# P written sorted by partition quarters, conversions by bit operations, a new order of stages, and eleven pairs transposed by VectorE

## The chip, the cores and the metric

The kernel runs on one core of a Trainium2 chip: TensorE (PE in the profile), VectorE (DVE), the scalar engine (ACT), GpSimd (POOL) and SyncE (SP), which issues all DMAs here. The metric is the device time of one execution in microseconds, lower is better. Before the change it was 659.45 us, the median of three runs (658.87 to 664.38).

## The reference

Three blocks stand in a row, all in float32, with B = 4, H = 12, S = 448, head width 64 and model width 768.

```python
# 1: causal attention, 48 heads
scores = (q @ k.T) / sqrt(64)                    # 448 x 448, -1e9 above the diagonal
x = softmax(scores) @ v                          # heads joined to (B, S, 768)
# 2: mixing
theta = x @ w_theta
y = w_tok_r @ (x * cos(theta)) + w_tok_i @ (x * sin(theta))
u = x + y;  x = u + relu(u @ w_ch)
# 3: four attention experts of width 64, two chosen per token by logits = x @ w_gate
out = sum over the two chosen e of  w_e * (softmax(scale * (x @ wq[e]) @ (x @ wk[e]).T) @ (x @ wv[e]) @ wo[e])
```

## The kernel before

Work is held with features on the partitions and the 448 tokens along the free dimension. Products that need float32 accuracy are made from a high and a low float32r part of each operand, three matmuls for one (`mm3`).

There are four stages for each batch b. `a` (`attn1`, line 753) is the attention of block 1, six pairs of heads. `m` (`mixing`, 794) is theta, sine and cosine, and the token matmuls of block 2. `p` (`project`, 857) is the product with w_ch and everything of block 3 that comes ahead of its scores: q, k, v and the gates. `c` (`attn2`, 962) is the attention of block 3, two pairs of experts, and the output product.

The attention of a pair is in `pair` (633). TensorE forms the scores in five PSUM banks of the tag tp. For each of seven pieces VectorE adds the mask and takes the row extreme (`softmax`, 646), ACT takes the exponential and its sum, and GpSimd or ACT scales with the reciprocal (`norm`, 673). The result is P, a tile `pa` of 128 x 2048, which is 16 blocks of 128 x 128. P must be transposed for the product with v. There are two ways. In the first TensorE transposes 16 blocks (`tp<-ident,pa`) and ACT or VectorE copies them out of PSUM to the tile `ph`. In the second (`by_dve`, for the pairs in the table `BYDVE`, nine before) VectorE transposes blocks of 32 x 32 in place, and 16 DMAs `ph<-pa` of 64 KB each move the blocks to their places, in runs of 32 elements, 128 bytes. The product P times V is `tp<-ph,vt` or `tp<-ph,v`.

The weights w_theta and w_ch and the token matrices arrive as float64. `widen` (570) makes a high and a low float32r half from the two 32-bit words of each number, for 24 halves of 384 columns (tile `c`) and 7 of 448 (tile `zt`). A converted half is kept in DRAM (`scr<-unit`) and loaded again for later batches (`unit<-scr`).

The order of the work is not written out. `Plan` records every operation; `Plan.issue` (322) then goes through time with assumed costs and issues on each engine the ready operation with the earliest due time. Due times come from the table `K`, the turn of each tile tag comes from `ORDER`, and where an operation has several engines to choose from (`either`, 283) the planner chooses. The instructions are emitted by one line, 498, so the profile is read by tile names. All engines go through their instructions in order.

Of the kernel before, what the change touches and what calls it, by code (L numbers as in the profile page):

```python
# [30 lines left out]
REBIAS = 2.0 ** -112  # L31
LOWBIT = 2.0 ** -52
NVG = E * D + E


class View:
# [16 lines left out]
    def rearrange(self, pattern, **sizes):  # L53
        left, right = (self._axes(side) for side in pattern.split("->"))
        known = dict(sizes)
        for group, n in zip(left, self.idx.shape):
            free = [a for a in group if a not in known]
            for a in free[:1]:
                known[a] = n // math.prod(known[x] for x in group if x != a)
        shape = [math.prod(known[a] for a in group) for group in right]  # L60
        return self._then(lambda ap: ap.rearrange(pattern, **sizes), self.idx.reshape(shape))

# [55 lines left out]
COLD = 7000.0  # L118
ISSUE = 380.0
SWITCH = 200.0  # L120
# [9 lines left out]
class Plan:  # L130
# [16 lines left out]
    def cost(self, engine, name, out, ins, kw):  # L147
# [14 lines left out]
        if engine == "vector":  # L162
            if name == "tensor_tensor_reduce":
                n = ins[0].width
            if name == "tensor_reduce":
                n = ins[0].width
            fast = name in ("tensor_scalar", "tensor_copy", "memset") and not psum and n >= 64
            return 68.0 + n * (0.521 if fast else 1.042)
# [130 lines left out]

    def scale(self, out, p, by):  # L300
        kw = {"scalar1": by, "scalar2": 1.0, "op0": OP.mult, "op1": OP.mult}
        self.either(("gpsimd", "tensor_scalar", (out, p), kw), ("scalar", "activation", (out, p, AF.Copy), {"scale": by}))

# [18 lines left out]
    def issue(self):  # L322
# [58 lines left out]
        count = 0  # L381
        port = dma_free = 0.0
        table = None
        mode = 0
        while count < len(self.steps):
# [13 lines left out]
            for e in order:  # L399
# [61 lines left out]
                if e == "sync":  # L461
                    dma_free = max(dma_free, end) + s.lag - 2200.0
                    done = dma_free + 2200.0
                s.at = (now, end)
                for u in s.heirs:
# [35 lines left out]
class Engine:  # L501
# [9 lines left out]
K = {"path": 2.0679528, "hop": -288.0949, "slack": 44.7258729, "war": 328.8541, "ahold": 262497.9943,  # L511
# [9 lines left out]


@with_exitstack
def dense_sparse_attention_kernel(ctx: ExitStack, tc: tile.TileContext, qk, v, w64, w32, wo, wvg, wtok, out):
# [9 lines left out]
    BUFS = {"unit": 6, "hl": 12, "zt": 6, "zn": 3, "xt": 2 * NK, "c1": 4, "raw": 3, "vt": 2,  # L534
            "qp": 3, "v2": 4, "pa": 2, "ph": 2, "cmb": 2, "st": 9, "gt": 2, "sm": 2}
    PBUFS = {"tp": 6, "mm": 2}
# [33 lines left out]
    def widen(raw, n, hi, lo, by=1.0):  # L570


        e_ = raw[:, :n, 1]
# [12 lines left out]
        plan.copy(hi, p_, "sgv")  # L586
        plan.combine(lo, p_, hi.f32(), OP.subtract, "gv")

# [44 lines left out]
    def pair(raw, vts, gate, dest, due, gap, by_dve):  # L633
# [9 lines left out]
        p_ = sbt([2048], F32, "pa")  # L643
        pc = p_[:, 768:1280]

        def softmax(sc_, p, n, m, col):
            dve.tensor_tensor_reduce(out=p, in0=sc_, in1=m, scale=-0.125, scalar=3.0e38,
                                     op0=OP.add, op1=OP.min, accum_out=bias[:, col:col + 1])
            act.activation(p, p, AF.Exp, bias=bias[:, col:col + 1], scale=-1.0, accum_out=sums[:, col:col + 1])

        def part(j, c):
            at = UNIT[c] * P + 128 * (c + 1) * j
            return p_[:, at:at + 128 * (c + 1)]

# [26 lines left out]
        got = scores()  # L681
        pool.memset(pc[:, S:], 0.0)
        soft(got, 2)
# [4 lines left out]
        plan.claim(p_)  # L688
        softmax(sc_[:, :S], pc[:, :S], S, mask3, 6)
        soft(got, 1)  # L690
        soft(got, 0)
        norm(2, 7, [(pc[:, :S], 6)] + [(part(j, c), 2 * (2 - c) + j) for c in (1, 0) for j in range(2)])
        plan.due = due + K["f2"] * gap

        pt = sbt([2048], F32, "ph")
        if by_dve:
            for at, n in ((0, 768), (768, 1280)):
                dve.transpose(p_[:, at:at + n], p_[:, at:at + n])
            plan.due = due + K["f4"] * gap
            for a in range(4):  # L700
                plan.group()
                for b_ in range(4):
                    block = p_.rearrange("p (u b k) -> p u b k", b=4, k=32)[32 * a:32 * a + 32, :, b_]
                    sp.dma_start(pt[32 * b_:32 * b_ + 32, 512 * a:512 * a + 512].rearrange("p (u q) -> p u q", q=32), block)
                plan.end_group()
# [6 lines left out]
        else:  # L712
# [3 lines left out]
            for i in range(4):  # L716
                tp = pst("tp")
                for n in range(4 * i, 4 * i + 4):
                    pe.transpose(tp[:, P * (n - 4 * i):P * (n - 4 * i + 1)], p_[:, P * n:P * n + P], ident)
                    if n == 0:  # L720
                        plan.claim(pt)
# [7 lines left out]

        plan.due = due + K["f3"] * gap  # L730
        o_ = pst("tp")
        hl = [sbt([S], F32R, "hl") for _ in range(2)] if dest is None else []
        plan.group()
# [305 lines left out]
```

## Time and profile before

| | |
|---|---|
| Median of three runs | 659.45 us (658.87 to 664.38) |
| Profiled execution | 663.81 us, span 662.0 us |
| TensorE / VectorE / ACT / GpSimd busy | 94% / 66% / 52% / 21% of the span |
| Granted TensorE clock, mean | 0.992 |
| DMA | 112.66 MB in 122,221 packets, 80,816 of them under 512 B |

Busy times are shares of the span, and the engines run beside each other, so they do not add up. The times of "idle before" count only the idle time of that engine just ahead of an instruction, and the name behind the arrow is what ended it. "SPq" is SyncE's issue of a DMA.

### The profile page before, as it was taken

The numbers are of one execution on the slowest core, as the hardware profiler recorded it, in microseconds if no ns is written. First come the engines' busy times: TensorE is split into PE (matmuls) and PEld (weight loads), VectorE is DVE, ScalarE is ACT, GpSimd is POOL, SyncE is SP. The second block draws the span as 40 slices with busy tenths as digits, with TensorE's granted clock in tenths as the row PEclk, the third lists the DMA queues.
The fourth block names the chain that finished last, engine by engine and source line by source line (L and its number), as shares of the span: only waits on it lengthen the run. The fifth ranks groups of instructions, "written<-read, shape, count | busy, mean of one in ns | idle before, by whom it ended". The sixth has DMA issues, their size and how long they took to land.

```text
span 662.0 us, 12525 instructions
## 1 busy us (share of the span) xinstructions
PE 621.5 (94%) x4352; PEld 535.4 (81%) x4352; DVE 435.4 (66%) x1319; ACT 345.6 (52%) x906; POOL 138.8 (21%) x252
## 2 busy tenths in 40 slices
PE   7989898999989999998889999989989999999987
PEld 5668577798879789887779889868879789999876
DVE  5989999943997986767442886656820768424260
ACT  5999898933362345756542552575721463101362
POOL 3465365401230011333120110113200120100010
PEclk9999999999999999998999999999999999999989
DMA  8667746204333787778778861267785873056325
GB/s 333 219 191 228 253 140 223 79 0 118 138 97 97 252 277 244 215 168 266 157 159 282 284 135 72 59 122 175 191 231 148 271 140 116 31 166 204 90 62 173
DMA packets 122221, 112.66 MB, mean 170 GB/s; under 512 B 80816, under 2 KB 92592, under 8 KB 122160
## 3 DMA queue, kind: packets, MB, share of 16 engines
q1 hardware_dynamic: 122160, 111.88, 57.4%
q8 instruction: 34, 0.56, 0.4%
q14 instruction: 27, 0.22, 0.1%
HBM read 81.15 MB, written 21.26 MB: 155 GB/s over the span
## 4 chain that ended last, share of the span: by engine, by line
PE 58%; DVE 15%; ACT 9%; SPq 7%; DMA 7%; issue 4%; POOL 0%; DVEq 0%; ACTq 0%; POOLq 0%
PE mm L498 42%; PE tp L498 17%; SPq L498 7%; ACT pa L498 6%; DVE zt L498 3%; DVE pa L498 3%; DVE cmb L498 3%; DMA unit<-scr 3%; DMA c<-scr 2%; DVE c L498 1%; DMA ph<-pa 1%; DMA out<-cmb 1%; DVE st L498 1%; DVE unit L498 1%; ACT ph L498 1%
## 5 line engine op out<-in xcount | busy, mean ns | idle before, releaser
L498 ACT ACTIVATE pa<-pa,st 128x128 f32<-128x128 f32 (+3 forms) x329 | 161.8, 516 | 56.4 <-DVE st L498 49.9
L498 PE MATMUL mm<-zt,unit 128*128 128x448 f32 x720 | 159.5, 374 | 1.9 <-DVE xt L498 1.9
L498 PEld LDWEIGHTS mm<-zt,unit 128*128 128x128 f32 x720 | 133.6, 188 | 18.2 <-issue 4.0
L498 PE MATMUL mm<-wt,zn 128*128 128x448 f32 x504 | 113.2, 373 | 2.4 <-ACT wt L498 1.2
L498 DVE CUSTOM_DVE_ANT_0 pa<-tp,mask 128x384 f32<-128x384 f32 (+3 forms) x224 | 87.9, 445 | 25.3 <-PE tp L498 25.2
L498 PEld LDWEIGHTS mm<-wt,zn 128*128 128x128 f32 x504 | 91.8, 188 | 12.2 <-DVE zn L498 1.6
L498 POOL TENSOR_SCALAR pa<-pa,st 128x384 f32<-128x384 f32 (+3 forms) x119 | 64.1, 554 | 170.2 <-DVE st L498 135.5
L498 PE MATMUL mm<-hl,unit 128*128 128x448 f32 x432 | 94.1, 373 | 2.8 <-DMA unit<-scr 1.1
L498 PEld LDWEIGHTS mm<-hl,unit 128*128 128x128 f32 x432 | 80.0, 188 | 13.8 <-ACT hl L498 1.5
L498 PE MATMUL tp<-raw 64*128 64x384 f32 (+3 forms) x336 | 63.6, 427 | 2.6 <-DVE st L498 1.1
L498 PE MATMUL tp<-ph,vt 128*64 128x128 f32 (+1 forms) x960 | 49.4, 264 | 12.9 <-issue 7.5
L498 PEld LDWEIGHTS tp<-ph,vt 128*64 128x64 f32 x960 | 45.8, 145 | 16.9 <-issue 8.7
L498 PE MATMUL tp<-ident,pa 128*128 128x128 f32 x368 | 50.9, 282 | 6.6 <-POOL pa L498 3.2
L498 PEld LDWEIGHTS tp<-ident,pa 128*128 128x128 f32 x368 | 43.0, 144 | 16.3 <-POOL pa L498 6.7
L498 PEld LDWEIGHTS tp<-raw 64*128 64x128 f32 (+1 forms) x336 | 34.9, 189 | 20.5 <-issue 4.3
L498 ACT ACTIVATE zn<-tp 128x512 fp32r<-128x512 f32 (+1 forms) x38 | 20.4, 546 | 52.5 <-PE tp L498 52.4
L498 ACT ACTIVATION_READ_ACCUMULATOR pa<-pa,st 128x1 f32 x224 | 42.3, 189 | 0.0
L498 DVE TENSOR_TENSOR zn<-tp,zn 128x512 fp32r<-128x512 f32 (+1 forms) x48 | 28.9, 620 | 16.9 <-ACT zn L498 16.6
L498 ACT ACTIVATE ph<-tp 128x512 f32<-128x512 f32 x62 | 33.2, 593 | 6.8 <-PE tp L498 6.6
L498 PE MATMUL mm<-unit,zt 128*128 128x260 f32 (+1 forms) x264 | 34.8, 286 | 0.5 <-DMA unit<-scr 0.3
L498 PEld LDWEIGHTS mm<-unit,zt 128*128 128x128 f32 (+1 forms) x264 | 33.1, 183 | 2.3 <-issue 1.0
L498 PE MATMUL tp<-hl,c 128*128 128x448 f32 x144 | 32.9, 372 | 1.3 <-DMA c<-scr 1.3
(115 smaller groups left out, 737.8 us busy)
## 6 DMA issues: line engine op xcount, KB each, us to landing
unit<-scr SPq DMA_DIRECT2D x96, 384.0 KB, 4.2
scr<-unit SPq DMA_DIRECT2D x32, 384.0 KB, 3.7
raw<-qk SPq DMA_DIRECT2D x24, 480.0 KB, 4.3
c<-w SPq DMA_DIRECT2D x24, 384.0 KB, 3.6
ph<-pa SPq DMA_DIRECT2D x144, 64.0 KB, 2.3
vt<-v SPq DMA_DIRECT2D x24, 256.0 KB, 3.6
unit<-scr SPq DMA_DIRECT2D x18, 260.0 KB, 3.2
c<-scr SPq DMA_DIRECT2D x18, 256.0 KB, 4.5
```

Source lines behind the costliest of these rows:

```text
L498: getattr(getattr(self.nc, engine), name)(*args, **kw)
```

## The change

It has five parts.

1. In a by_dve pair P is written sorted by partition quarters: the columns of the 16 blocks are laid out by their quarter of 32 first and by block second. VectorE then transposes two halves of 1024 columns (before 768 and 1280), and each of the 16 moves takes 512 contiguous elements of 32 partitions, runs of 2 KB. In such a pair the mask pass writes back into PSUM and the exponential reads from there; the 64 unused columns of the last block are filled in PSUM by VectorE, where GpSimd filled them in SBUF.
2. `widen` joins the bits of the two words by shift and or, where it made the mantissa with a multiply-add in PSUM and a multiply.
3. `ORDER` goes batch by batch (m1 behind c0, and so on), and `K` is new.
4. `BYDVE` has two more pairs, 3 and 5 of batch 1, eleven in all.
5. The planner's model: an issue costs 400 ns, at most 8 DMAs are on their way, a cost for transposes on VectorE. Pools: qp 3 to 2 buffers, v2 4 to 2, and a separate tag hc (4) for the output of block 3's attention.

```diff
-BYDVE = {"a0": (), "a1": (), "a2": (0, 2, 4), "a3": (0, 2, 4), "c0": (0,), "c1": (0,), "c2": (0,), "c3": ()}
-ORDER = ["a0", "m0", "a1", "m1", "p0", "c0", "a2", "p1", "m2", "c1", "a3", "p2", "m3", "c2", "p3", "c3"]
+BYDVE = {"a0": (), "a1": (3, 5), "a2": (0, 2, 4), "a3": (0, 2, 4), "c0": (0,), "c1": (0,), "c2": (0,), "c3": ()}
+ORDER = ["a0", "m0", "a1", "p0", "c0", "m1", "a2", "p1", "c1", "m2", "a3", "p2", "c2", "m3", "p3", "c3"]
...
-        dve.tensor_scalar(p_.bitcast(U32), e_, 3, 0x7F800000, op0=OP.logical_shift_left, op1=OP.bitwise_and)
+        u_ = p_.bitcast(U32)
+        dve.tensor_scalar(u_, e_, 3, 0x7FFFFFFF, op0=OP.logical_shift_left, op1=OP.bitwise_and)
         plan.claim(hi)
-        dve.scalar_tensor_tensor(p_.bitcast(U32), e_, 0x80000000, p_.bitcast(U32), op0=OP.bitwise_and, op1=OP.bitwise_or)
-        dve.tensor_scalar(e_, e_, 0xFFFFF, None, op0=OP.bitwise_and)
-        x_ = pst("tp")[:, :n]
-        act.activation(x_, e_, AF.Copy, scale=by * 2.0 ** -20, bias=by)
-        y_ = e_.bitcast(F32)
-        dve.scalar_tensor_tensor(y_, raw[:, :n, 0].bitcast(U32), by * LOWBIT, x_, op0=OP.mult, op1=OP.add)
-        plan.combine(p_, y_, p_, OP.mult, "vg")
-        plan.copy(hi, p_, "sgv")
-        plan.combine(lo, p_, hi.f32(), OP.subtract, "gv")
+        dve.scalar_tensor_tensor(u_, r_, 29, u_, op0=OP.logical_shift_right, op1=OP.bitwise_or)
+        dve.scalar_tensor_tensor(u_, e_, 0x80000000, u_, op0=OP.bitwise_and, op1=OP.bitwise_or)
+        if by == 1.0:
+            plan.copy(hi, p_, "sgv")
+            plan.combine(lo, p_, hi.f32(), OP.subtract, "gv")
+        else:
+            plan.scale(hi, p_, by, "sgv")
+            dve.scalar_tensor_tensor(lo, p_, by, hi.f32(), op0=OP.mult, op1=OP.subtract)
...
+        by_key = p_.rearrange("p (b u k) -> p u b k", b=4, k=32)
...
+            x = sc_[:, :n] if by_dve else p
+            dve.tensor_tensor_reduce(out=x, in0=sc_[:, :n], in1=m, scale=-0.125, scalar=3.0e38,
                                      op0=OP.add, op1=OP.min, accum_out=bias[:, col:col + 1])
+            if by_dve:
+                x = sc_.rearrange("p (u b k) -> p u b k", b=4, k=32)
+            act.activation(p, x, AF.Exp, bias=bias[:, col:col + 1], scale=-1.0, accum_out=sums[:, col:col + 1])
...
-            for at, n in ((0, 768), (768, 1280)):
-                dve.transpose(p_[:, at:at + n], p_[:, at:at + n])
+            for at in (0, 1024):
+                dve.transpose(p_[:, at:at + 1024], p_[:, at:at + 1024])
...
-                    block = p_.rearrange("p (u b k) -> p u b k", b=4, k=32)[32 * a:32 * a + 32, :, b_]
-                    sp.dma_start(pt[32 * b_:32 * b_ + 32, 512 * a:512 * a + 512].rearrange("p (u q) -> p u q", q=32), block)
+                    sp.dma_start(pt[32 * b_:32 * b_ + 32, 512 * a:512 * a + 512], p_[32 * a:32 * a + 32, 512 * b_:512 * b_ + 512])
```

The pair 2 of batch 3 stands on SyncE's queue before like this (`unit` are halves of weights, `raw` the queries and keys of a pair, `vt` its values):

```order
L498 DMA raw_5096<-qk 128x960
L498 DMA unit_5100<-scr_0_500_2641 128x768
L498 DMA unit_5130<-scr_1_506_2663 128x768
L498 DMA vt_5221<-v 128x512
L498 DMA vt_5247<-v 128x512
L498 DMA raw_5276<-qk 128x960
L498 DMA unit_5280<-scr_0_513_2699 128x768
L498 DMA ph_5285<-pa_5152 32x16x32 x16
L498 DMA out<-cmb_5302 128x448
```

and with the change like this:

```order
L508 DMA raw_5046<-qk 128x960
L508 DMA unit_5053<-scr_0_387_1970 128x768
L508 DMA unit_5067<-scr_1_393_2003 128x768
L508 DMA unit_5107<-scr_0_388_1982 128x768
L508 DMA vt_5134<-v 128x512
L508 DMA ph_5138<-pa_5010 32x512 x16
L508 DMA unit_5242<-scr_1_395_2011 128x768
L508 DMA unit_5247<-scr_0_400_2052 128x768
L508 DMA unit_5256<-scr_1_407_2086 128x768
```

The 16 moves stand at a like place, in another shape: 512 elements in one run for each of 32 partitions, where there were 16 runs of 32. On VectorE the first converted half of w_theta (tile `c`, result `cmb`) stood among other work in these rows before:

```order
L498 TENSOR_SCALAR cmb_361<-c_14_103 128x384
L498 RECIPROCAL st_321<-st_321 128x5
L498 SCALAR_TENSOR_TENSOR cmb_361<-c_14_103,cmb_361 128x384
L498 COPY xt_330<-tp_329 128x448
L498 TENSOR_SCALAR c_14_103<-c_14_103 128x384
L498 TENSOR_TENSOR hl_402<-xt_330,hl_397 128x448
L498 TENSOR_SCALAR cmb_409<-c_21_123 128x384
L498 SCALAR_TENSOR_TENSOR c_14_103<-c_14_103,tp_404 128x384
```

and with the change in these:

```order
L508 TENSOR_SCALAR cmb_297<-c_17_112 128x384
L508 COPY xt_270<-tp_269 128x448
L508 SCALAR_TENSOR_TENSOR cmb_297<-c_17_112,cmb_297 128x384
L508 CAST hl_323<-xt_270 128x448
L508 SCALAR_TENSOR_TENSOR cmb_297<-c_17_112,cmb_297 128x384
```

The mask and the multiply-add with PSUM (`tp_404`) are gone, and a second bit operation stands in their place. The mask passes of the same pair 2 of batch 3 (`ISA`, into `pa` before) begin with the change like this:

```order
L508 MEMSET tp_5017 128x64
L508 ISA tp_5006,st_5024<-tp_5006,mask_67 128x384
L508 ISA st_5024 128x1
L508 ISA tp_5007,st_5024<-tp_5007,mask_67 128x384
L508 ISA st_5024 128x1
L508 ISA tp_5008,st_5024<-tp_5008,mask_67 128x256
```

They write into the PSUM banks that they read, and the fill of the last bank stands ahead of them.

## Rows read from the trace of the kernel before

**Rows 1.** The page: span, and busy time, share and instructions of each engine.

```profile
span 662.0 us, 12525 instructions
...
PE 621.5 (94%) x4352; PEld 535.4 (81%) x4352; DVE 435.4 (66%) x1319; ACT 345.6 (52%) x906; POOL 138.8 (21%) x252
```

**Rows 2.** Chain that ended last: start, duration (us), what, count.

```profile
151.03 1.31 PE tp L498 x12
...
582.47 36.80 PE mm L498 x180
...
650.70 4.87 DMA c<-scr
```

**Rows 3.** Stretches: us, busy of each engine (count), TensorE clock, DMA share, GB/s.

```profile
60.00:130.00 70.00, 63.30 (x521) 50.83 (x521) 68.85 (x198) 61.73 (x156) 32.44 (x42) 1.00 0.58 187
...
285.00:345.00 60.00, 53.96 (x436) 45.90 (x434) 36.00 (x126) 35.28 (x104) 17.45 (x34) 0.94 0.76 185
...
430.00:490.00 60.00, 54.32 (x513) 45.52 (x513) 37.02 (x127) 37.55 (x111) 13.80 (x30) 1.00 0.70 165
```

**Rows 4.** Groups by shape: busy, mean ns | idle before and what ended it.

```profile
L498 PE MATMUL tp<-ph,vt 128*64 128x128 f32 x576 | 42.1, 288 | 12.9 <-issue 7.5 <-ACT pa L498 2.7 <-DMA ph<-pa 2.1
```

**Rows 5.** What TensorE waited for: us in total, times, longest.

```profile
PE tp L498 <- issue: 7.5, 4, 2.5
...
PE tp L498 <- DVE zt L498: 4.1, 4, 1.8
...
PE mm L498 <- DVE xt L498: 1.9, 2, 1.5
...
PE mm L498 <- DMA unit<-scr: 1.4, 3, 0.7
...
PE tp L498 <- DMA c<-scr: 1.3, 1, 1.3
```

**Rows 6.** SyncE in order of time: start, duration (us), operation, count.

```profile
284.74 13.80 SPq L498 DMA_DIRECT2D ph<-pa  x16
...
431.24 11.83 SPq L498 DMA_DIRECT2D ph<-pa  x16
```

**Rows 7.** DMA issues by tile: count, KB each, median us to landing.

```profile
ph<-pa SPq DMA_DIRECT2D x144, 64.0 KB, 2.3
...
out<-cmb SPq DMA_DIRECT2D x18, 224.0 KB, 2.9
```

**Rows 8.** By tile, SyncE: duration of an issue in ns (min/median/max).

```profile
L498 SPq DMA_DIRECT2D ph<-pa x144: 585/631/3442, 271.7 to 543.6; - x144
...
L498 SPq DMA_DIRECT2D raw<-qk x24: 327/333/591, 0.7 to 449.8; - x24
```

**Rows 9.** Stretches of 4 us behind two waits; the fraction is the granted clock.

```profile
300.00:304.00 4.00, 3.69 (x48) 3.72 (x50) 0.99 (x7) 2.08 (x10) 0.00 (x0) 0.61 0.92 330
...
328.00:332.00 4.00, 4.00 (x64) 4.00 (x62) 1.02 (x2) 0.54 (x1) 0.00 (x0) 0.57 1.03 340
```

**Rows 10.** Groups by shape, conversions and transposes of VectorE and ACT.

```profile
L498 DVE SCALAR_TENSOR_TENSOR cmb<-c,cmb 128x384 uint32<-128x384 uint32 x24 | 14.4, 602 | 0.1
...
L498 DVE STREAM_TRANSPOSE pa<-pa 128x1280 f32<-128x1280 f32 x9 | 13.6, 1509 | 1.7 <-ACT pa L498 1.6
...
L498 DVE SCALAR_TENSOR_TENSOR c<-c,tp 128x384 f32<-128x384 uint32 x24 | 13.0, 548 | 1.1 <-ACT tp L498 0.9
...
L498 ACT ACTIVATE tp<-c 128x384 f32<-128x384 uint32 x24 | 12.5, 524 | 21.4 <-DVE c L498 21.2
...
L498 DVE TENSOR_TENSOR cmb<-c,cmb 128x384 f32<-128x384 f32 x19 | 11.1, 591 | 0.0
...
L498 DVE TENSOR_SCALAR c<-c 128x384 uint32<-128x384 uint32 x24 | 10.1, 423 | 0.1
```

**Rows 11.** The page, groups: exponentials and scalings of ACT, and its readouts.

```profile
L498 ACT ACTIVATE pa<-pa,st 128x128 f32<-128x128 f32 (+3 forms) x329 | 161.8, 516 | 56.4 <-DVE st L498 49.9
...
L498 ACT ACTIVATION_READ_ACCUMULATOR pa<-pa,st 128x1 f32 x224 | 42.3, 189 | 0.0
```

More of the change, by code (lines that the diff above doesn't have):

```diff
@@ L31 @@
 REBIAS = 2.0 ** -112
-LOWBIT = 2.0 ** -52
 NVG = E * D + E
@@ L60, in rearrange @@
         shape = [math.prod(known[a] for a in group) for group in right]
-        return self._then(lambda ap: ap.rearrange(pattern, **sizes), self.idx.reshape(shape))
+        flat = [a for group in left for a in group]
+        cells = self.idx.reshape([known[a] for a in flat]).transpose([flat.index(a) for group in right for a in group])
+        return self._then(lambda ap: ap.rearrange(pattern, **sizes), cells.reshape(shape))
     @staticmethod
@@ L118 @@
 COLD = 7000.0
-ISSUE = 380.0
+ISSUE, LANES = 400.0, 8
 SWITCH = 200.0
@@ L166, in cost @@
                 n = ins[0].width
+            if name == "transpose":
+                return 66.0 + 1.13 * n
             fast = name in ("tensor_scalar", "tensor_copy", "memset") and not psum and n >= 64
@@ L298, in copy, with scale @@
         self.either(*(forms[e] for e in engines))
-    def scale(self, out, p, by):
+    def scale(self, out, p, by, engines="gs"):
         kw = {"scalar1": by, "scalar2": 1.0, "op0": OP.mult, "op1": OP.mult}
-        self.either(("gpsimd", "tensor_scalar", (out, p), kw), ("scalar", "activation", (out, p, AF.Copy), {"scale": by}))
+        forms = {"g": ("gpsimd", "tensor_scalar", (out, p), kw), "v": ("vector", "tensor_scalar", (out, p), kw),
+                 "s": ("scalar", "activation", (out, p, AF.Copy), {"scale": by})}
+        self.either(*(forms[e] for e in engines))
     def combine(self, out, a, b, op, engines="gv"):
@@ L382, in issue @@
         port = dma_free = 0.0
+        landed = []
         table = None
@@ L463, in issue @@
                     done = dma_free + 2200.0
+                    landed += [done - i * ISSUE for i in range(len(calls))][::-1]
+                    if len(landed) >= LANES:
+                        busy[e] = max(end, landed[-LANES])
+                        heapq.heappush(wake, busy[e])
                 s.at = (now, end)
@@ L534, in dense_sparse_attention_kernel @@
     BUFS = {"unit": 6, "hl": 12, "zt": 6, "zn": 3, "xt": 2 * NK, "c1": 4, "raw": 3, "vt": 2,
-            "qp": 3, "v2": 4, "pa": 2, "ph": 2, "cmb": 2, "st": 9, "gt": 2, "sm": 2}
+            "qp": 2, "v2": 2, "hc": 4, "pa": 2, "ph": 2, "cmb": 2, "st": 9, "gt": 2, "sm": 2}
     PBUFS = {"tp": 6, "mm": 2}
@@ L570, in widen @@
     def widen(raw, n, hi, lo, by=1.0):
-        e_ = raw[:, :n, 1]
+        e_, r_ = raw[:, :n, 1], raw[:, :n, 0].bitcast(U32)
         act.activation(e_.f32(), e_.f32(), AF.Copy, scale=REBIAS)
@@ L643, in pair, with part @@
         p_ = sbt([2048], F32, "pa")
-        pc = p_[:, 768:1280]
+        by_key = p_.rearrange("p (b u k) -> p u b k", b=4, k=32)
+        def part(j, c):
+            at = UNIT[c] + (c + 1) * j if c < 3 else UNIT[c]
+            if by_dve:
+                return by_key[:, at:at + c + 1]
+            return p_[:, at * P:at * P + (128 * (c + 1) if c < 3 else S)]
         def softmax(sc_, p, n, m, col):
-            dve.tensor_tensor_reduce(out=p, in0=sc_, in1=m, scale=-0.125, scalar=3.0e38,
+            x = sc_[:, :n] if by_dve else p
+            dve.tensor_tensor_reduce(out=x, in0=sc_[:, :n], in1=m, scale=-0.125, scalar=3.0e38,
                                      op0=OP.add, op1=OP.min, accum_out=bias[:, col:col + 1])
[L649 to L653, printed above, removed]
+            if by_dve:
+                x = sc_.rearrange("p (u b k) -> p u b k", b=4, k=32)
+            act.activation(p, x, AF.Exp, bias=bias[:, col:col + 1], scale=-1.0, accum_out=sums[:, col:col + 1])
         def scores():
@@ L681, in pair @@
         got = scores()
-        pool.memset(pc[:, S:], 0.0)
         soft(got, 2)
@@ L688, in pair @@
         plan.claim(p_)
-        softmax(sc_[:, :S], pc[:, :S], S, mask3, 6)
+        if by_dve:
+            dve.memset(sc_[:, S:], -0.125 * MASKED)
+        else:
+            pool.memset(p_[:, UNIT[3] * P + S:(UNIT[3] + 4) * P], 0.0)
+        softmax(sc_, part(0, 3), S, mask3, 6)
         soft(got, 1)
         soft(got, 0)
-        norm(2, 7, [(pc[:, :S], 6)] + [(part(j, c), 2 * (2 - c) + j) for c in (1, 0) for j in range(2)])
+        norm(2, 7, [(part(0, 3), 6)] + [(part(j, c), 2 * (2 - c) + j) for c in (1, 0) for j in range(2)])
         plan.due = due + K["f2"] * gap
@@ L719, in pair @@
                     pe.transpose(tp[:, P * (n - 4 * i):P * (n - 4 * i + 1)], p_[:, P * n:P * n + P], ident)
-                    if n == 0:
+                    if n == 4 * i:
                         plan.claim(pt)
@@ L728, in moving @@
                 return pt[:, at:at + P]
-        plan.due = due + K["f3"] * gap
+        plan.due = due + K["g3" if by_dve else "f3"] * gap
         o_ = pst("tp")
-        hl = [sbt([S], F32R, "hl") for _ in range(2)] if dest is None else []
+        hl = [sbt([S], F32R, "hc") for _ in range(2)] if dest is None else []
         plan.group()
```

3 lines of the change are left out of this document (2 added, 1 removed), and 18 rows, old and new, of the table K.

## The prediction

> **What bounds the kernel now.** I read the engine totals first, then the stretches, then what TensorE waited for, then the queue of SyncE, and last the forms of the instructions that the change touches. TensorE is busy 621.5 of 662.0 us [rows 1], so only what adds to its work or leaves it idle counts. Busy overstates the work, because a matmul's record is longer than its slot: steady stretches give 36.80/180 = 0.204 us for a matmul of 448 columns and 1.31/12 = 0.109 us for a transpose of a 128x128 block [rows 2]. Pricing every matmul of TensorE's row at such steady slots gives some 576 us. The other 86 us are lost in four places: some 35 in the first 130 us, 9 from there to 285, 26 from 285 to 490, and 16 from 490 to the end (an estimate, from counts times those slots).
>
> The stretches [rows 3] say what limits each. In 60 to 130 us VectorE is busy 68.85 of 70: it sets the pace there. In 285 to 345 and in 430 to 490 no compute engine is full and TensorE is busy 53.96 and 54.32 of 60. What it waits for there stands in its own row: the first matmul of P times V sat idle for 12.9 us [rows 4], put down to "issue", a DMA and ACT [rows 5]. All of these are the same thing: the moves ph<-pa. A pair that VectorE transposes needs 16 of them, and SyncE spends 13.80 and 11.83 us to issue one set [rows 6]. The 2.7 us put down to ACT belongs here too: that set ran from 431.24 to 443.07, landing takes 2.3 us [rows 7], and TensorE went on at about 445.6.
>
> **The moves.** One issue of ph<-pa takes 631 ns, one of raw<-qk 333 ns [rows 8]. The first cuts its 64 KB into 512 runs of 128 bytes, the second moves 128 runs. The change makes 32 runs of 2 KB of each move. No row has so few runs; between 631 (no gain) and 333 I take 333, since it is the nearest in runs, plus the 0.1 us that the queue leaves between two issues (11.83/16 - 0.631). A set then takes 16 x 0.43 = 6.9 us rather than 12 to 14, so P is there some 5 us sooner, and the five waits between 2.0 and 2.7 us, and the smaller ones, all fit into that. The order also puts more work in front of most of the P times V matmuls: priced at steady slots, TensorE's work between a pair's scores and its P times V was 16.5 to 53 us (six of nine below 21), and is 18.6 to 72 (three of eleven below 22). I take 12.0 of the 12.9 us. Two pairs more go this way, 32 issues, at 0.43 us each 14 us of SyncE, against 144 x 0.31 = 45 us that it is spared; the loads of weights and of raw stand behind fewer microseconds of moves than before.
>
> With the waits goes a second loss. In the 4 us after two of them the granted clock was 0.61 and 0.57 [rows 9]: TensorE had stood idle and then ran part of the stretch at the lower of its two levels. That is 4 x (0.39 + 0.43) = 3.3 us of clock; I take 3.0.
>
> Against this stands a rule of the Trainium skill (DMA: Bandwidth & Descriptors, "Why small descriptors are slow (HBM only)"): transfers from SBUF to SBUF do not suffer from small descriptors. By it longer runs win nothing, the 15 us are not there, and the sum is 652. The trace agrees for the landing (2.3 us for the moves, 2.9 for out<-cmb, whose runs are longer [rows 7]) and not for the queue, where the issue takes twice as long.
>
> **Transposes.** Two pairs fewer on TensorE take away 2 x 16 x 0.109 = 3.5 us of a full engine. In their place VectorE works: two passes per pair, 22 of 1024 columns for 18, at 1.51 us for 1280 and so about 1.2 each [rows 10], 5 us in all, against copies out of PSUM that go.
>
> **The conversions and the first 130 us.** A float64 half loses on VectorE a mask (423 ns), a multiply-add (548) and a multiply (591), and gains one bit operation like the one that stays (602): 0.96 us less, and ACT loses 524 ns [rows 10]. There are 31 of them, 19 in the first 130 us, so 18 us are taken from VectorE there. Not all of it comes back as time, since the new order also asks for more at once: project 0 comes before mixing 1, and the token matmuls begin after 68 us of TensorE's work rather than 81. I counted VectorE's instructions up to the last one that TensorE's row needs, each at its row's busy time over its count. In the old order they run ahead of TensorE's own work by at most 29 us, in the new by 25.5; ACT's lead falls from 22 to 13. What is lost there is then 31 rather than 35. So I take 3.5 us; the ends are 0 (VectorE is full anyway and the order asks for as much) and 13 (the 18 us less the 5 of the two added pairs). Over the whole run TensorE waits 1.9 and 4.1 us for VectorE's xt and zt [rows 5]; with shorter chains I take 2.0 of these, between 0 and 6.
>
> **The end.** 1.3 us of waiting for c<-scr [rows 5, 2]: the new order asks for two of these tiles after the last pairs, the old for four. I take 1.0.
>
> **What it adds.** A pair of VectorE's now keeps its scores in PSUM until ACT has read them, where the mask pass freed the bank before; five of the six banks named tp are held for longer. I take 2.0 us for this over 11 pairs; the ends are in the rivals. The VectorE fill that replaces GpSimd's stands ahead of the mask passes in seven pairs and waits for a bank, at places where VectorE is idle four tenths of the time: nothing. The smaller pools (qp, v2) and the separate tag hc: nothing, or part of the rivals.
>
> **Sum.** The profiled execution took 663.81 us, its span 662.0. 12.0 + 3.0 + 3.5 + 3.5 + 2.0 + 1.0 - 2.0 = 23.0 us, so 640.8. The median of the runs shown, 659.45, is 0.9934 of the profiled execution, so the forecast is 637 us, 3.4% less. Its own range, from the bounds, is 629 to 645.
>
> **Rivals.**
> - *The moves stay as slow*, because an issue costs by something else than its runs. For it: no row shows 32 runs. Against it: the two rows on issue [rows 8]. The 15 us are not won: 652 us. Chance 0.10. It is the outcome that the Trainium skill's rule above gives.
> - *The first 130 us pay in full.* VectorE is at 98% in 60 to 130 us, so 13 us rather than 3.5 could come back, and the conversions of project 0 likewise run faster: about 625 us. Against it is the count of what the new order asks for. Chance 0.12.
> - *The order makes waits of its own.* More matmuls stand in stretches where two output groups alternate (957 against 637 in the orders), and each such stretch has two halves of weights live at once. TensorE waits for unit<-scr 1.4 us in all, at most 0.7 at once [rows 5]; the 320 matmuls are 18 pairs of halves, at 0.7 each 13 us: 650 us. Chance 0.11.
> - *PSUM becomes the bound, and it is slower.* The next pair's scores need four banks that ACT must have read. Seven exponentials at 161.8/329 = 0.49 and seven readouts at 0.19 us are 4.8 us [rows 11]. If ACT is at other work when the scores arrive, TensorE, which goes in order, stands still for up to that. In 11 pairs that is 53 us, and the time 690; it decides from 2.1 us per pair, where it has eaten the gain. Against it: ACT is busy only about 0.6 of the time in these stretches, and 4 to 9 us of other matmuls stand between most such scores and the next. Chance 0.07.
>
> The forecast keeps 0.60. A measurement of this kernel can tell about 1% from no change. Faster by over 1% means below 652.9: the forecast, the second rival, two thirds of the third (0.07) and half of the first (0.05), 0.84. The rest of these two is within 1%, 0.09. Slower is 0.07. The range 623 to 654 takes in the first three rivals nearly whole and leaves the fourth out.
>
> **What will show it.** An issue of ph<-pa near 333 ns, and a set in 6 to 7 us; idle time before P times V under 2 us; no stretch of 285 to 490 us with a granted clock below 0.9; some 336 transposes of pa; VectorE still at 95% or more before the token matmuls, with the loss there near 31 us. I am wrong if TensorE's waits name ACT or the scores' banks, if issues stay above 0.5 us, or if the first 130 us change by more than 8 us.

## The result and the profile after

The changed kernel takes 634.03 us, the median of four runs (632.69 to 635.42), against 660.65 for the kernel before in the same session (658.87 to 664.38): a ratio of 0.959, interval 0.954 to 0.964. The forecast was 637 us, its range 623 to 654.

The page of the kernel after, for [rows 1]:

```profile
span 630.9 us, 12382 instructions
...
PE 607.5 (96%) x4320; PEld 525.7 (83%) x4320; DVE 424.1 (67%) x1294; ACT 327.0 (52%) x869; POOL 119.8 (19%) x219
```

The stretches of the kernel after, for [rows 3]:

```profile
60.00:130.00 70.00, 63.91 (x445) 52.42 (x441) 69.85 (x176) 51.89 (x124) 30.33 (x34) 1.00 0.43 140
285.00:345.00 60.00, 58.23 (x516) 48.61 (x516) 42.07 (x160) 41.19 (x130) 15.21 (x30) 1.00 0.66 194
430.00:490.00 60.00, 60.00 (x529) 52.19 (x525) 38.56 (x143) 34.08 (x106) 8.68 (x22) 1.00 0.58 177
```

TensorE went from 53.96 to 58.23 and from 54.32 to 60.00 of 60 us in the two later stretches, at full clock. In 60 to 130 us VectorE is as full as before. The first row of P times V by shape, for [rows 4]:

```profile
L508 PE MATMUL tp<-ph,vt 128*64 128x128 f32 x576 | 39.6, 276 | 0.0
```

All of its 12.9 us of idle time is gone. What TensorE still waits for (us in total, times, longest), for [rows 5]:

```profile
PE tp L508 <- POOL pa L508: 4.4, 5, 2.5
PE mm L508 <- POOL ident masks.py:199: 2.5, 1, 2.5
PE tp L508 <- DVE zn L508: 2.4, 2, 1.3
PE tp L508 <- ACT ph L508: 2.0, 1, 2.0
PE mm L508 <- DMA unit<-scr: 2.0, 2, 1.6
```

But the moves are not what the forecast made of them. SyncE in order of time, for [rows 6]:

```profile
287.69 11.56 SPq L508 DMA_DIRECT2D ph<-pa  x16
```

An issue of a move in ns (min/median/max) and its time to landing in us, for [rows 8, 7]:

```profile
L508 SPq DMA_DIRECT2D ph<-pa x176: 507/588/1815, 106.0 to 515.2; - x176
...
DMA to landing us min/median/max: 1.9/2.0/6.2
```

An issue takes 588 ns where 333 was forecast, and a set, from its first issue to its last, 10.1 to 14.2 us where 6.9 was. The waits went, the sets hardly changed: that is the question of the experiments.

VectorE's rows by shape in the first 165 us of the kernel after, for [rows 10]:

```profile
L508 DVE SCALAR_TENSOR_TENSOR cmb<-c,cmb 128x384 uint32<-128x384 uint32 x48 | 26.0, 566 | 0.2
L508 DVE TENSOR_SCALAR cmb<-c 128x384 uint32<-128x384 uint32 x24 | 9.8, 413 | 0.1
L508 DVE SCALAR_TENSOR_TENSOR cmb<-zt,cmb 128x448 uint32<-128x448 uint32 x14 | 9.1, 663 | 0.0
L508 DVE TENSOR_SCALAR cmb<-zt 128x448 uint32<-128x448 uint32 x7 | 2.7, 380 | 0.0
```

All 31 conversions (24 + 7) are done by then; in the kernel before it was 19:

```profile
L498 DVE SCALAR_TENSOR_TENSOR cmb<-c,cmb 128x384 uint32<-128x384 uint32 x12 | 6.8, 570 | 0.0
L498 DVE SCALAR_TENSOR_TENSOR cmb<-zt,cmb 128x448 uint32<-128x448 uint32 x7 | 4.9, 693 | 0.0
```

### The profile page after: what moved, and what is told of

It reads as the page before. It is cut to its first block, busy times and chain, and to the rows that moved or that the text cites. A ratio compares the mean times of both kernels' runs of the same rounds, so it can differ in the third digit from the quotient of the medians.

```text
span 630.9 us, 12382 instructions
## 1 busy us (share of the span) xinstructions
PE 607.5 (96%) x4320; PEld 525.7 (83%) x4320; DVE 424.1 (67%) x1294; ACT 327.0 (52%) x869; POOL 119.8 (19%) x219
## 4 chain that ended last, share of the span: by engine, by line
PE 70%; DVE 9%; DMA 3%; ACT 2%; SPq 1%; issue 1%; POOL 0%; DVEq 0%; ACTq 0%; POOLq 0%
PE mm L508 50%; PE tp L508 20%; DVE zt L508 3%; DMA unit<-scr 2%; DVE pa L508 2%; DVE cmb L508 2%; SPq L508 1%; ACT pa L508 1%; DVE st L508 1%; DVE tp L508 1%; DMA c<-scr 1%; DVE zn L508 1%; DMA vt<-v 0%; ACT L508 0%; POOL pa L508 0%
## 5 line engine op out<-in xcount | busy, mean ns | idle before, releaser
L508 ACT ACTIVATE pa<-pa,st 128x128 f32<-128x128 f32 (+4 forms) x257 | 125.0, 516 | 44.5 <-DVE st L508 34.9
L508 PEld LDWEIGHTS mm<-zt,unit 128*128 128x128 f32 x720 | 133.9, 188 | 15.9 <-issue 4.0
L508 PE MATMUL mm<-wt,zn 128*128 128x448 f32 x504 | 117.3, 375 | 0.4 <-DVE st L508 0.4
L508 PE MATMUL mm<-hl,unit 128*128 128x448 f32 x432 | 97.8, 376 | 3.9 <-DMA unit<-scr 2.0
L508 DVE CUSTOM_DVE_ANT_0 pa<-tp,mask 128x384 f32<-128x384 f32 (+3 forms) x147 | 58.6, 444 | 10.6 <-PE tp L508 10.4
L508 PE MATMUL tp<-ident,pa 128*128 128x128 f32 x336 | 45.3, 277 | 8.4 <-POOL pa L508 4.4
L508 ACT ACTIVATE pa<-tp,st 128x256 f32<-128x256 f32 (+3 forms) x77 | 37.7, 510 | 27.2 <-DVE st L508 27.1
L508 PEld LDWEIGHTS tp<-ident,pa 128*128 128x128 f32 x336 | 37.9, 141 | 15.9 <-POOL pa L508 7.4
L508 PEld LDWEIGHTS tp<-raw 64*128 64x128 f32 (+1 forms) x336 | 34.1, 190 | 16.9 <-issue 4.7
L508 PEld LDWEIGHTS tp<-ph,vt 128*64 128x64 f32 x960 | 42.3, 137 | 4.7 <-issue 2.8
L508 ACT ACTIVATE zn<-tp 128x384 fp32r<-128x384 f32 (+1 forms) x33 | 17.7, 541 | 48.7 <-PE tp L508 47.2
L508 DVE TENSOR_TENSOR zn<-tp,zn 128x512 fp32r<-128x512 f32 (+1 forms) x48 | 29.1, 618 | 17.8 <-ACT zn L508 17.6
L508 DVE SCALAR_TENSOR_TENSOR xt<-mm,xt 128x448 f32<-128x448 f32 x24 | 15.0, 624 | 28.9 <-PE mm L508 28.6
```

The lines of the kernel that those rows point to most:

```text
L508: getattr(getattr(self.nc, engine), name)(*args, **kw)
```

## The experiments

Theory at the start: the new order hides a set of 11 us behind other work of TensorE, so the moves' price no longer matters; the shorter conversions are worth a part of VectorE's time. Rivals: the longer runs did it, or the conversions did. Eight of the kernels keep the order of every engine as it was and change one price or two, so that time is not mixed with a new layout; four are laid out anew by the planner. All ratios are to the kernel before, run beside them, and a gain in us that has an interval is worked out from its ratio.

| kernel | us | ratio (interval) | TensorE idle before P times V, us |
|---|---|---|---|
| before, order kept, 4 moves | 644.0 | 0.976 (0.973 to 0.979) | 0.6 |
| before, order kept, 2 KB runs | 648.59 | 0.982 (0.979 to 0.986) | 4.5 |
| the same, quarters reversed | 648.59 | 0.985 (0.982 to 0.988) | 3.6 |
| before, order kept, light conversion | 653.58 | 0.991 (0.988 to 0.994) | 12.8 |
| before, order kept, light and 2 KB | 641.07 | 0.972 (0.968 to 0.975) | 4.3 |
| after, order kept, 4 moves | 633.36 | 0.959 (0.956 to 0.961) | 0.2 |
| after, order kept, 128-byte runs | 642.03 | 0.972 (0.969 to 0.974) | 2.3 |
| after, order kept, 30 us more VectorE | 662.41 | 1.004 (1.002 to 1.006) | 0.0 |
| after, nine pairs | 635.39 | 0.963 (0.961 to 0.965) | 0.0 |
| order alone | 664.99 | 1.007 (1.005 to 1.010) | 6.1 |
| all but the order | 673.96 | 1.020 (1.015 to 1.024) | 12.2 |
| before, new conversion, laid out anew | 675.74 | 1.026 (1.021 to 1.030) | 14.0 |

**Four moves in place of 16**, in the kernel after and in the kernel before.

```diff
-                for b_ in range(4):
-                    sp.dma_start(pt[32 * b_:32 * b_ + 32, 512 * a:512 * a + 512], p_[32 * a:32 * a + 32, 512 * b_:512 * b_ + 512])
+                sp.dma_start(pt[:, 512 * a:512 * a + 512], p_[:, 512 * a:512 * a + 512])
```

The lines taken out are those of the kernel after. In the kernel before, the moves that go are those in runs of 128 bytes, so there the edit also makes the runs 2 KB long.

> The changed kernel with its order kept, but the 16 moves of a set (32 partitions x 2 KB each) made 4 of 128 partitions x 2 KB with the same bytes in all. The 32x32 blocks then stay in their partition quarter, so P is not fully transposed: that part of the computation is left out. What is asked: what does an issue of a move cost, and does the length of a set still decide anything? If an issue costs what it costs for any transfer of 128 rows of one partition each (333 to 400 ns, as raw and vt), a set is 1.5 to 2 us. If an issue between two places in SBUF is dear as such (590 ns), it is 2.4 to 2.8 us. My theory (the new order hides a set of 11 us wholly): the time stays within 3 us of 634, since TensorE's idle time before P times V is 0.0 already. Rival (queue: loads of weights behind the moves on SyncE are still late): 9 us of queue less per set lets the unit loads come earlier, and the 2.0 us of waits for unit and some of the rest go: 629 to 631.

> The kernel before with its order kept and the same edit: 4 moves of 128 partitions x 2 KB in place of 16 of 32 partitions x 16 runs of 128 bytes, so P is not fully transposed. My theory (the waits before P times V and the dips of the clock behind them came from the 11 to 14 us that SyncE spends on a set): a set falls to 2 or 3 us, TensorE's idle time before P times V falls from 12.9 to under 2 us, no stretch of 285 to 490 us has a clock below 0.95, and the time falls by 12 to 16 us, from 660.6 to 645 to 649. Rival (the queue is not what is late there; the P itself, its exponentials and transposes, come late, and the set is only the last name in the chain): it falls by under 6 us, 655 to 660, and TensorE waits for VectorE or ACT at the same places.

An issue in the first and in the second of these kernels, ns (min/median/max):

```profile
L509 SPq DMA_DIRECT2D ph<-pa x44: 465/592/1302, 106.5 to 506.8; - x44
```

```profile
L499 SPq DMA_DIRECT2D ph<-pa x36: 470/551/1435, 270.0 to 518.3; - x36
```

A move in runs of 2 KB between two places in SBUF costs SyncE some 0.55 to 0.6 us, with 32 partitions or 128, 64 KB or 256: a set of four is short because it has four issues (2.4 to 3.5 us where nothing stands between them). In the old order the edit is worth 15.9 us (interval 13.9 to 17.8), at the upper end of what was expected; its stretches and its waits before P times V:

```profile
285.00:345.00 60.00, 60.00 (x551) 51.71 (x548) 37.60 (x133) 37.37 (x109) 17.50 (x34) 1.00 0.67 211
...
430.00:490.00 60.00, 60.00 (x516) 52.41 (x514) 30.52 (x105) 31.81 (x92) 10.98 (x21) 1.00 0.57 180
```

```profile
L499 PE MATMUL tp<-ph,vt 128*64 128x128 f32 x576 | 39.1, 276 | 0.6 <-DVE st L499 0.6
```

So the moves were what was late in the kernel before, and the forecast's 15 us for the waits and the clock behind them were the right size for taking them away. These 15.9 us are not the price of twelve issues alone: with 16 moves in runs of 2 KB, the next experiment, 11.6 of them are already won, and 4.3 are left (the difference of the two ratios). In the new order, where the runs are 2 KB on both sides, four moves are worth 0.7 us, by medians and within the spread: the length of a set no longer decides.

**The runs alone.** The change's own line for the moves in the kernel before, and the old line in the kernel after (order kept in both):

```diff
 before, 2 KB runs:
-                    block = p_.rearrange("p (u b k) -> p u b k", b=4, k=32)[32 * a:32 * a + 32, :, b_]
-                    sp.dma_start(pt[32 * b_:32 * b_ + 32, 512 * a:512 * a + 512].rearrange("p (u q) -> p u q", q=32), block)
+                    sp.dma_start(pt[32 * b_:32 * b_ + 32, 512 * a:512 * a + 512], p_[32 * a:32 * a + 32, 512 * b_:512 * b_ + 512])
 after, 128-byte runs: the reverse
```

> The changed kernel with its order kept, but each move reads and writes 16 runs of 128 bytes per partition, as before the change, in place of one of 2 KB. The elements come to other places, so P times V is not the reference's. My theory (runs decide neither the issue nor the time): an issue stays between 560 and 640 ns, TensorE's idle time before P times V stays under 1 us, the time is 632 to 637. Rival A (my prediction's step, issue goes with the runs): an issue goes up from 588 by more than 100 ns. Rival B (the 73,728 short packets hold up the DMA engines, and with them the loads of weights): 638 to 645, with waits for unit or raw in TensorE's row.

> The kernel before with its order kept on every engine, and only the moves changed from 16 runs of 128 bytes per partition to one of 2 KB. The elements come to other places, so P times V is not the reference's. Putting short runs back into the changed kernel cost 8 us there, with an issue at 628 ns instead of 588 and 5.8 us of waits for unit instead of 2.0. Theory 1 (short runs cost through the DMA engines, which then bring the weights late, in either order): 8 us less here too, 650 to 654. Theory 2 (they cost where the order has loads of weights close behind the moves, as the new one has): 2 to 4 us less, 655 to 659, from the 40 ns of 16 issues and earlier landings in front of P times V.

Issue, and P times V, of the kernel before with 2 KB runs:

```profile
L498 SPq DMA_DIRECT2D ph<-pa x144: 507/588/1762, 271.1 to 528.7; - x144
```

```profile
L498 PE MATMUL tp<-ph,vt 128*64 128x128 f32 x576 | 39.3, 275 | 4.5 <-ACT pa L498 2.3 <-issue 1.6 <-DVE st L498 0.6
```

Its stretch from 285 us:

```profile
285.00:345.00 60.00, 57.53 (x541) 49.16 (x540) 36.65 (x128) 36.35 (x106) 17.56 (x34) 1.00 0.70 211
```

One of its sets on SyncE, behind the same set in the kernel before:

```profile
313.21 11.96 SPq L498 DMA_DIRECT2D ph<-pa  x16
```

```profile
308.61 11.79 SPq L498 DMA_DIRECT2D ph<-pa  x16
```

And the kernel after with 128-byte runs, its issues and what TensorE waited for:

```profile
L508 SPq DMA_DIRECT2D ph<-pa x176: 585/628/1956, 109.4 to 525.2; - x176
```

```profile
PE mm L508 <- DMA unit<-scr: 5.8, 4, 3.6
...
PE tp L508 <- ACT pa L508: 2.3, 2, 1.6
```

16 times fewer runs make an issue only 40 ns shorter, so my theory that runs decide neither the issue nor the time falls in its second half: the runs are worth 11.6 us (9.3 to 13.9) in the old order and, by the difference of the two ratios, 8 us in the new one (medians 642.03 and 634.03). Rival B of the first text had it. Theory 1 of the second had nearly the size (its range began at 650) but not the mechanism: weights that come late were only 1.4 us of waits in the old order. The idle time before P times V fell from 12.9 to 4.5 us, 8.4, and the granted clock of 285 to 345 us rose from 0.94 to 1.00, 0.06 x 60 = 3.6 us. Five of the waits of the old order were 2.0 to 2.7 us each, the others under 1. Measured from the start of VectorE's last pass to the end of SyncE's last issue, the sets of the kernel before took 11.8 to 16.8 us (nine sets), with 2 KB runs 11.0 to 14.3, each 0.6 to 3.8 us less; landing fell from 2.3 to 2.0 us. That is about as long as the waits were. In the new order the short runs bring the weights late (unit 5.8 us for 2.0) and two of the P times V.

The DMA engines say the same. The page's line on the queue (packets, MB, share of 16 engines' span), of the kernel before and of the kernel before with 2 KB runs:

```profile
q1 hardware_dynamic: 122160, 111.88, 57.4%
```

```profile
q1 hardware_dynamic: 53040, 111.88, 55.0%
```

0.574 x 662.0 - 0.550 x 646.2 = 24.6 us of all 16 engines less for the same bytes. The Trainium skill (DMA: Bandwidth & Descriptors, "Why small descriptors are slow (HBM only)") says that transfers from SBUF to SBUF do not suffer from small descriptors; here they do, by these numbers.

**When a set begins.** With 2 KB runs the first moves of a set need only one of VectorE's two passes, and five of the nine sets began before the second ended, four of them by up to 1.4 us, the last, whose issues are spread, by 3.6.

```diff
-                for b_ in range(4):
+                for b_ in (3, 2, 1, 0):
```

> As the kernel before with moves of 2 KB runs, order kept, but the four moves of each group go in the other order of quarters (3, 2, 1, 0 in place of 0, 1, 2, 3), so P times V is again not the reference's. A move of 2 KB from quarters 0 and 1 reads only what VectorE's first transpose pass has written, while a move in 128-byte runs reads both passes; so the sets with 2 KB runs began up to 1.4 us before the second pass ended. With quarter 3 first, each set waits for the second pass again; runs, issue and landing stay. Theory 1 (most of the 11.5 us came from the earlier begin, which took the waits of 2.0 to 2.7 us below what is late next): the six sets begin 1.1 to 1.4 us later against the end of the transposes, the idle time before P times V goes from 4.5 up to 7 to 10 us, and the time is 651 to 655. Theory 2 (it came from the runs, through quicker issues, landings and free DMA engines): idle time stays at 4 to 6 us and the time within 1.5 us of 648.6.

It took the same 648.59 us. The edit did only part of what it was to do: in the order that is kept, VectorE makes the wider pass first in three of the nine pairs, and there quarter 3 begins early instead. The set above, in this kernel, does begin with the second pass:

```profile
309.14 11.08 SPq L498 DMA_DIRECT2D ph<-pa  x16
```

VectorE's second pass ends at 309.12 us here and at 309.77 in the kernel with the quarters in order. Counted from that end, the set begins 1.19 us later than there and its last issue ends 0.47 us later: of 1.2 us of early begin, 0.7 were spent on waiting inside the set. Theory 1 fails in the sum (idle 3.6 us, not 7 to 10); what the early begin alone is worth pair by pair stays open.

**VectorE's time, in the new order.**

```diff
+        again("vector", "tensor_scalar", u_, e_, 3, 0x7FFFFFFF, op0=OP.logical_shift_left, op1=OP.bitwise_and)
...
+        again("vector", "scalar_tensor_tensor", u_, e_, 0x80000000, u_, op0=OP.bitwise_and, op1=OP.bitwise_or)
```

> The changed kernel with its order kept on every engine, and in each of the 31 conversions two of VectorE's bit operations done twice, 31 x (413 + 566 ns) = 30.3 us more of VectorE, 18.6 of them in the first 130 us. It asks what the shorter conversion is worth in this order. Theory 1 (my prediction's step: VectorE sets the pace of the first 130 us, but only a part comes back): +3 to +8 us, 637 to 642, with the loss in the first 130 us up from 28.7 to 32 to 36. Theory 2 (every microsecond of VectorE there is a microsecond of the whole): +16 to +20, 650 to 654. Theory 3 (hidden, the order decides): under +2, 632 to 636.

662.41 us, 28.4 us more than the kernel after: more than any of the three theories. Theory 2 has the mechanism but counts too few conversions: all 31 stand ahead of 165 us and not 19, as the count that I took over from the old order had it. Matmul by matmul the two traces are 6.6 us apart at 60 us of the kernel after, 21.6 at 120 and 28.8 at 160, and 28.0 from 200 to 600. Its stretches:

```profile
60.00:130.00 70.00, 56.21 (x406) 44.68 (x406) 69.06 (x181) 48.90 (x123) 26.51 (x33) 0.95 0.35 115
130.00:285.00 155.00, 144.78 (x926) 127.46 (x925) 120.62 (x316) 65.33 (x157) 22.27 (x36) 0.99 0.57 182
```

VectorE is as full, and TensorE has 56.21 instead of 63.91 us. In the new order a microsecond of VectorE ahead of 165 us is 0.95 us of the whole (28.8 of 30.3). That includes a lower granted clock, 0.95 and 0.99 in these stretches where the kernel after has 1.00: 0.05 x 70 + 0.01 x 155 = some 5 us.

**VectorE's time, in the old order.** The mask, ACT's scaling and the multiply-add take 8 columns; the planner still sees them whole.

```diff
         dve.tensor_scalar(e_, e_, 0xFFFFF, None, op0=OP.bitwise_and)
+        plan.narrow()
         act.activation(x_, e_, AF.Copy, scale=by * 2.0 ** -20, bias=by)
+        plan.narrow()
         dve.scalar_tensor_tensor(y_, raw[:, :n, 0].bitcast(U32), by * LOWBIT, x_, op0=OP.mult, op1=OP.add)
+        plan.narrow()
```

> The kernel before with its order kept on every engine, and in each of the 31 conversions the mask, the scaling on ACT and the multiply-add narrowed to 8 columns of 384 or 448, so the converted numbers are wrong. Takes about 26 us from VectorE and 15 us from ACT, as the new conversion takes 30 and 16. Laid out anew, the new conversion made the old kernel slower (675.7 us); this asks what it is worth while the order stands still. In the new order 30 us of VectorE cost 28. Theory 1 (VectorE sets the pace of the first 130 us in either order, all 17 us that fall there come back, or more): 636 to 645. Theory 2 (my prediction's step: about a fifth comes back): 653 to 658. Theory 3 (nothing, the old order has room): 658 to 662.

The edit takes less than was expected, since an instruction of 8 columns is not free; the narrowed forms and the page's totals of this kernel:

```profile
L502 DVE TENSOR_SCALAR c<-c 128x8 uint32<-128x8 uint32 x24 | 5.6, 234 | 0.1
...
L502 DVE SCALAR_TENSOR_TENSOR c<-c,tp 128x8 f32<-128x8 uint32 x24 | 3.6, 155 | 0.7 <-ACT tp L502 0.7
```

```profile
PE 616.5 (95%) x4352; PEld 532.7 (82%) x4352; DVE 420.1 (65%) x1319; ACT 334.3 (52%) x906; POOL 139.2 (21%) x252
```

VectorE is 435.4 - 420.1 = 15.3 us lighter, ACT 11.3, and 6.2 us come back (4.3 to 8.1). The time falls into theory 2's range, but only because the edit was smaller; theory 2 had a fifth. The 15.3 us do not all stand where VectorE sets the pace, since here 12 of the 31 conversions come behind 165 us. The kernel before up to 165 us, and this one up to the same work of every engine:

```profile
0.00:165.00 165.00, 149.76 (x1192) 121.61 (x1193) 131.77 (x413) 125.08 (x328) 66.31 (x115) 1.00 0.55 178
```

```profile
0.00:158.50 158.50, 147.06 (x1192) 121.10 (x1193) 123.02 (x413) 118.22 (x328) 66.69 (x115) 1.00 0.56 186
```

There VectorE is 8.75 us lighter and TensorE 6.5 us earlier, 0.7 per us; the rest of the saving brings some 2 us by 285 us, matmul by matmul in the two traces. ACT is 6.9 us lighter there too, and what of the 6.5 us is its part was not tried apart. The idle time before P times V is unchanged.

```profile
L502 PE MATMUL tp<-ph,vt 128*64 128x128 f32 x576 | 42.0, 287 | 12.8 <-issue 6.5 <-ACT pa L502 3.9 <-DMA ph<-pa 1.7
```

> Both of these edits at once on the kernel before, order kept: the old order with about the new prices of moves and conversions (wrong numbers for the same two reasons). The difference from 634 is what the new order with its two more pairs brings at equal prices. Theory 1 (at the new prices the new order is worth the waits before P times V, 10 us and more): 644 to 655. Theory 2 (the prices alone do it, the order only had to be laid out anew for them): 632 to 640.

Both together bring 18.7 us (16.2 to 21.2), near the sum of 6.2 and 11.6: in the old order the two act in different places. From 641.07 to 634.03, 7 us, is left to the new order with its two pairs, and in it to the half of the conversion's saving that the narrowed one does not have. 641 lies between the two theories' ranges, so neither is shown. At equal prices the new order may be worth nothing: if 15 of the 30 us that were put onto VectorE above cost half of the 28, an estimate, it would take some 648 us at the prices of this kernel.

**Parts laid out anew.** Here the planner makes a new order from the due times named.

```diff
 order alone: the kernel after with the old widen, the old pair layout and
-"a1": (3, 5)
+"a1": ()
 all but the order: the kernel after with the old ORDER, K, pools and planner's costs
 before, new conversion: the kernel before with the new widen and scale
```

> The new order of stages, the new due times, the planner's model and the pools (parts 3 and 5), with the old conversion, the old layout of P with its runs of 128 bytes, and nine pairs. The planner lays the order out anew, with due times that were found for the changed kernel. Theory 1 (order decides: batch by batch there is more work of TensorE between the scores and P times V): TensorE's idle time before P times V is under 3 us though the sets still take 11 us and more, and the time is 638 to 648. Theory 2 (the shorter conversion decides, and with the old one the new order asks VectorE for too much in the first 130 us): the loss there rises from 34.7 to 40 and more, the waits before P times V are gone, and the time is 648 to 662.

> Parts 1, 2 and 4 (sorted P with runs of 2 KB, conversion by bit operations, eleven pairs by VectorE) with the old order of stages, the old due times, costs of the planner and pools. Theory 1 (order decides; a set still takes 11 us and nothing more stands in front of P times V): the waits there stay at 8 us or more, and grow with the two more pairs; what is won is 3.5 us of transposes and 3 to 8 of the conversions: 648 to 657. Theory 2 (the shorter moves and conversions decide): 636 to 644.

> The kernel before with the new conversion alone (part 2); the planner lays it out anew with the old due times. It takes 30 us from VectorE and 16 from ACT. Theory 1 (VectorE paces the first 130 us, part of it comes back): 653 to 657, the loss in the first 130 us down from 34.7 by 3 to 7. Theory 2 (hidden): 658 to 662. Theory 3 (in full): 640 to 647.

All three are slower than the kernel before, and the last two lie above the ranges of all their theories. By the prediction's count (real time less TensorE's work at steady slots, an estimate), what is lost once TensorE has done 100 us of work is 34.5 us before, 28.9 after, 41.7 for the order alone, 32.3 for all but the order, 30.9 for the old kernel with the new conversion. So the new order without the cheap conversion loses 7 us more there (theory 2, and its time a little above its range), and its moves nearly stop mattering though its sets take 10.8 to 14.4 us:

```profile
L509 PE MATMUL tp<-ph,vt 128*64 128x128 f32 x576 | 42.6, 288 | 6.1 <-DMA vt<-v 4.3 <-issue 1.2 <-DMA ph<-pa 0.5
```

4.3 of these 6.1 us are a load of values, not moves. The new conversion in the old kernel wins its 3.6 us ahead of 130 us, as theory 1 had it, and gives back more later: the loss is 63.6 us at 300 us of work (57.8 before) and 79.3 at 400 (66.4). TensorE waits there in all:

```profile
PE tp L500 <- DMA ph<-pa: 7.9, 3, 3.3
...
PE mm L500 <- DMA unit<-scr: 3.9, 2, 3.1
PE tp L500 <- issue: 3.6, 2, 1.8
PE mm L500 <- issue: 3.4, 1, 3.4
```

With the order kept, the narrowed conversion, with half the saving, made the same kernel 6 us faster; laid out anew with due times that were found for other prices, the new one made it 16.9 us slower. These three runs therefore measure the fit of the due times more than the part they were to measure, and the 16.9 us are no price of the conversion.

**Nine pairs.**

```diff
-"a1": (3, 5)
+"a1": ()
```

> The changed kernel with nine pairs by VectorE in place of eleven (part 4 undone): pairs 3 and 5 of batch 1 go through TensorE's transposes again, and the planner lays it out anew. My theory: 32 transposes of 0.109 us come back to an engine that is full, +3.5 us, and the copies out of PSUM load ACT and VectorE: 636 to 641. Rival (the two pairs stand in the first 130 to 285 us, where VectorE paces; VectorE and SyncE are relieved of two pairs): 630 to 635, no loss or a gain.

635.39 us, 1.4 more by medians and with intervals that overlap: what the two more pairs are worth is told neither from nothing nor from the 3.5 us of the forecast. The trace leans to the rival in part: from 130 to 285 us TensorE is busy for all of 155.00 us, where it is for 152.70 with eleven pairs, and the 2.4 us of waits for zn are gone.

## Why the prediction was right, point by point

- **The moves (12.0) and the clock behind them (3.0).** The size was right, in part by luck: idle time before P times V went from 12.9 to 0.0, and no stretch from 285 to 490 us has a clock under 1.00, but the sets did not become as short as the sum has them. The step that failed is "between 631 (no gain) and 333 I take 333, since it is the nearest in runs": an issue takes 588, a set 10.1 to 14.2 us and not 6.9. The row was nearest in runs but not in kind, since raw<-qk comes from DRAM; whether that is what makes its issue short is not shown, and some other loads from DRAM took 382 to 512 (unit<-scr, c<-wo in the kernel before). In its place two other things took the waits away. The sets end 0.6 to 3.8 us sooner, by longer runs, which in the old order took 8.4 of the 12.9 us; shorter issues are only 16 x 43 ns = 0.7 us of a set, and what the rest is made of stays open. And the new order takes nearly all by itself: with 128-byte runs it leaves 2.3. That it does so by putting more work in front is the count that the text gave beside it; no run moves that work alone. The prediction had made "issues above 0.5 us" a sign that it was wrong; it was a sign of the wrong step only, since no wait was longer than 2.7 us.
- **The rival "moves stay as slow", 652 us.** Its premise came true and its time did not, because it let the waits hang on the issue alone. The Trainium skill's rule that stands beside it, by which longer runs win nothing, does not hold here: they win 11.6 us in the old order and 8 in the new.
- **The first 130 us (3.5) and "pay in full" (625).** Measured by the same count, 34.7 became 28.7, 6.0 us, where 31 was forecast. "The new order also asks for more at once" was the right reason: it pulls 12 more conversions ahead of 165 us and spends there what they became cheaper. How much of VectorE's time comes back hangs on the order as well as on the conversion: ahead of 165 us it was 0.7 us per us taken away in the old order, with ACT lightened too, and 0.95 per us added in the new, the clock included.
- **Transposes (3.5).** 336 of them, as forecast; undoing the two pairs costs 1.4 us by medians, which is no change clear of the spread.
- **VectorE's xt and zt (2.0), the end (1.0).** (In block 2, xt are the features, zt their products with sine and cosine, and zn is zt transposed.) The waits for xt (1.9) are gone and those for zt fell from 4.1 to 1.1 on the same row; against that stand 2.4 us for zn that were not there before its transposes, and 1.7 for zt before matmuls, where there were 0.5. c<-scr fell from 1.3 to 0.5.
- **PSUM banks (-2.0 and the rival at 690).** The scores' matmuls, tp<-raw, which sat idle for 2.6 us, sit idle for 0.0, so no wait names their banks. Waits for VectorE's st ahead of tp, which stood at 4.1 us, are 0.8. This term was not needed.
- **The order makes waits of its own (650).** It did, in one way that the forecast left out: not in the two-group stretches but in that it leans on the cheap conversion and on runs of 2 KB. With 30 us more of VectorE it is 28 us slower, with the short runs 8. With both old prices and nine pairs, laid out anew, it took 664.99, but that also measures due times that were found for other prices.

The sum came out 3 us from the median with some luck in it. The set was mis-sized, yet its term came true by the longer runs and the new order. Between the two profiled executions the span fell by 31.1 us (662.0 to 630.9) where 23.0 was forecast: the first 130 us paid 2.5 more, the 2.0 for PSUM did not come, and the rest is not traced to a cause. The medians fell by 26.6, since the profiled execution of the kernel before, 663.81, lay above its median.

## What to carry to other kernels

Price an edit with the order held still before you let a scheduler lay it out anew: here a cheaper conversion made the kernel 6 us faster one way and 17 slower the other. A wait of 2 us at the end of a chain of 14 goes when the chain becomes 2 us shorter, so ask how long the single waits are before you ask how much shorter the chain must become. And a cheaper step and a new order are one change: the order decides where the saving is spent.

## What the runs showed of the hardware

- SyncE's issue of a DMA between two places in SBUF took 0.55 to 0.63 us in every shape tried (32 runs of 2 KB 588 ns, 512 runs of 128 bytes 628 to 631, 128 runs of 2 KB 551 to 592; medians). In the kernel before, loads and stores of DRAM took between 0.32 and 0.51 (scr<-unit 327, raw<-qk 333, unit<-scr 382, c<-wo 512). What makes the difference was not tried apart.
- Runs of 128 bytes between places in SBUF cost the DMA engines time against runs of 2 KB: 24.6 us of all 16 over 144 moves, and 0.3 us of landing.
- VectorE instructions of 8 columns took 155 to 234 ns, where those of 384 took 423 and 548.
